# A spectral filter and token MLP, forward and backward: places of some loads, slots and stores changed

## The chip, the core and the metric

The kernel runs on one core of one Trainium2 chip. The metric is the device time of one execution in microseconds (us), here the median of three runs. The engines are PE (matmuls; PEld is its weight load), DVE (vector), ACT (scalar and activations), POOL (it also issues DMAs) and SP (it issues DMAs only).

## What is computed

Forward: a layer norm, a two-dimensional FFT filter over sequence and features, a residual, a second layer norm and a token-mixing MLP, with its residual. Backward: the gradients of all seven inputs that count. The kernel has eight outputs: h2, then the gradients of x, w_r, w_i, w1, b1, w2 and b2 (out_0 to out_7).

```python
def _A_ref(x, w_r, w_i):                      # B, S, D = 1, 2048, 448
    X = jnp.fft.rfft2(x.astype(jnp.float32), axes=(-2, -1))
    X = X * (w_r + 1j * w_i)                  # w_r, w_i: 2048 x 225
    return jnp.fft.irfft2(X, s=(S, D), axes=(-2, -1)).astype(jnp.bfloat16)

def _B_ref(x, w1, b1, w2, b2):                # w1: 2048 x 1792, w2: 1792 x 2048
    h = _layernorm(x, axis=-1)
    u = _gelu(jnp.einsum("bsd,sf->bdf", h, w1) + b1)
    y = jnp.einsum("bdf,fs->bds", u, w2) + b2
    return y.transpose(0, 2, 1)

h = x + _A_ref(_layernorm(x), w_r, w_i)
h2 = h + _B_ref(_layernorm(h), w1, b1, w2, b2)
# and the vector-Jacobian product of all this with grad_out
```

## The kernel before

**Stages, in order of time.** (1) x comes in four pieces of four rows each (`load_x`, L295). Each group is normed (`Norm`, L356 on) and goes through `fft_rows` (L403): DVE folds it into `eo` (L406, L407, L411), PE multiplies it with the table `kf` (L417), ACT or DVE put the result into `zt` (`ev`, L283, L284). (2) Beside this PE has a large, independent product: `dg(j)` (L606), for 14 blocks j of 128, adds up sixteen matmuls (L610) of a block of w2, transposed, with the natural grad_out (`go_nat`). Each block is loaded by a DMA that transposes (`load_w2T`, L325, by `ld_t`, L232) into a ring of four buffers (`w4`), and `dg(j)` asks for the next block at its end. The scheduler puts dg's matmuls between the others to fill PE. (3) `fft_cols` (L436, then L455 and L460 into `xs`), a complex product with w_r and w_i on DVE (`cmul`, L510 to L513, from `w_t`), and the inverse, `ifft_cols` (L534, with the table `hi`; ACT copies one half, L551, DVE adds and subtracts, L553). (4) Rows back (`rows_mid` and `rows_out`, L578 to L590, with `di0` and `kinv`), the residual and the second norm; stores to `hn_d` and `hln_d`. (5) The MLP: w1 in natural layout (L683), the activation and its derivative, w2 in natural layout (L752) with the result h2 stored from L757 on. (6) Backward through w1: sixteen blocks of w1, transposed by DMA into the same ring, L811, and the norm's backward pass (`norm_back`, L770 to L784). (7) The backward FFT with `zt2`, `ds`, `ab2`. Between its steps run the gradients of w2 (`gw2`, from `goT` and `g_t`) and w1 (`gw1`, from `hlnT` and `du_t`), by `halves` (full matmuls at L259, tails on 64 rows at L266). The last four rows of the gradient of w1 run by themselves at the end (L939 on).

**What sets the order.** Each engine and each DMA queue works in its own order; a scheduler makes that order, and semaphores join the queues. `nxt` (L237) chains loads on SP: each is issued behind the one before it in the text. So SP's order in the first part is the order of the calls: x, go_nat, x, go_nat, one w2T, x, x, three w2T, then (L614 to L628) one w2T from `dg(0)`, df1, hf twice, w_t four times, three w2T, hi, di0, kinv, ident. Most stores, and some loads, are issued by POOL (`st`, L229, and L226 with `po`), in their order. `slot(i, ...)` names one of eight large buffers, s0 to s7. A tile in a slot waits until the tile before it there is used up. w2's quarters (`w2c`, L734 to L745) lie in slots 0, 2, 4 and 6; later `g_t` is in 0, `zt2` and then `du_t` in 2, `goT` and then `xs_b` in 4. PSUM has pools m0 and m1 (`ps_mm` takes them in turn) and sp (`ps_sp`), of two, two and four banks.

**The lines that the steps touch.**

```python
    load_x(0)                                   # L298
...
    def ld_t4(out, in_):                        # a transposed load in two DMAs
        ld_t(out[:, 0:3, :], in_[:, 0:384])
        ld_t(out[:, 3, :], in_[:, 320:448])
...
    st(out_7.rearrange("(q h) -> q h", h=NT), gb2b[:])      # L865, on POOL
```

`gb2b` holds sums that ACT makes of the sixteen rows of `go_r` (L766, L768); `go_r` is grad_out again, by rows, in slot 5.

Of the kernel before, what the change touches and what calls it, by code (L numbers as in the profile page):

```python
# [17 lines left out]
P = 128  # L18
S = 2048
D = 448  # L20
DF = 225
F = 1792
NFB = 14
NT = 16
NR = 32
NJ = 16
XW = NJ * DF
# [137 lines left out]
def kernel(  # L165
# [20 lines left out]
    nc = tc.nc  # L186
    ve, ac, po, pe = nc.vector, nc.scalar, nc.gpsimd, nc.tensor
# [7 lines left out]
    def slot(i, shape, name):  # L195
        return big.tile(shape, BF16, tag=f"s{i}", name=name)

    def w4(shape, name):
        return ring.tile(shape, BF16, tag="w4", bufs=4, name=name)
# [15 lines left out]
    def ps_m(k, shape, dtype=F32):  # L215
        return psum.tile(shape, dtype, tag=f"m{k}", bufs=2, name=f"ps_m{k}")

    def ps_mm(shape, dtype=F32):
        turn.append(len(turn) // 2 % 2)
        return ps_m(turn[-1], shape, dtype)  # L220
# [4 lines left out]
    def ld(out, in_, eng=None):  # L225
        return (eng or nc.sync).dma_start(out=out, in_=in_)  # L226

    def st(out, in_, eng=None):
        return (eng or po).dma_start(out=out, in_=in_)  # L229

    def ld_t(out, in_):
        return nc.sync.dma_start(out=out, in_=in_, transpose=True)  # L232
# [4 lines left out]
    def nxt(load, *args):  # L237
        if chain:
            with tc.issue_after(chain[-1].ins):
                chain.append(load(*args))  # L240
        else:
            chain.append(load(*args))

    def ld_t4(out, in_):

        ld_t(out[:, 0:3, :], in_[:, 0:384])
        ld_t(out[:, 3, :], in_[:, 320:448])
# [33 lines left out]
    def ev(out, in_, on):  # L281
        if on == "a":
            return ac.copy(out=out, in_=in_)  # L283
        return ve.tensor_copy(out=out, in_=in_)  # L284
# [4 lines left out]
    def rows(ap):  # L289
        return ap.rearrange("(q h) d -> q h d", h=NT)  # L290
# [4 lines left out]
    def load_x(g):  # L295
        nxt(ld, x[:, 4 * g:4 * g + 4, :], rows(A_x[0])[:, 4 * g:4 * g + 4, :])
# [16 lines left out]
    def table(shape, src, tag=None):  # L313
        t = consts.tile(shape, BF16, name=src, **({"tag": tag} if tag else {}))
        nxt(ld, t[:], hnd[src].ap())
        return t

    def load_w(dst, on):
        for c, w in enumerate((A_w_r, A_w_i)):
            for b in range(2):  # L320
                on(ld, dst[64 * b:64 * b + 64, c, :], by_half(w)[b])
# [3 lines left out]
    def load_w2T():  # L325
        j = len(w2T)
        if j < NFB:
            w2T.append(w4([P, NT, P], "w2T"))
            nxt(ld_t, w2T[j][:], B_w2[j * P:(j + 1) * P, :])


    go_nat = slot(6, [P, NT, D], "go_nat")
    for g in range(2):
        nxt(ld, go_nat[:, 8 * g:8 * g + 8, :],
            grad_out[0].rearrange("(t p) d -> p t d", p=P)[:, 8 * g:8 * g + 8, :])
        if g == 0:
            load_x(1)
    load_w2T()
    load_x(2)
    load_x(3)  # L340
    for j in range(3):
# [61 lines left out]
    def fft_rows(src, zt, g, on, behind=None, twice=False):  # L403
        eo = e4([P, 4, D], "eo")
        a, b = src[:, 4 * g:4 * g + 4, 1:224], src[:, 4 * g:4 * g + 4, 447:224:-1]
        ve.tensor_tensor(out=eo[:, :, 1:224], in0=a, in1=b, op=ALU.add)  # L406
        ve.tensor_tensor(out=eo[:, :, 225:448], in0=a, in1=b, op=ALU.subtract)  # L407
        if twice:
            eo = fold_2(eo, src, g)
        else:  # L410
            ve.tensor_copy(out=eo[:, :, 0:225:224], in_=src[:, 4 * g:4 * g + 4, 0:225:224])  # L411
        for i in range(4):
            h = 4 * g + i
            pz = ps_sp([P, 4, P])
            with tc.issue_after(behind.ins) if behind is not None else nullcontext():
                for c, o in enumerate((0, 113, 226, 322) if twice else (0, 97, 225, 320)):
                    last = pe.matmul(pz[:, c, :], lhsT=eo[:, i, o:o + P], rhs=kf[:, c // 2 * P:c // 2 * P + P],  # L417
                                     start=True, stop=True)
            done = ev(zt[:, :, :, 4 * h:4 * h + 4], pz[:, :, :].rearrange("p c (s k) -> p c s k", k=4), on[i])
        return last, done  # L420
# [185 lines left out]
    def dg(j):  # L606
        pg = ps_m(0, [P, D])
        with tc.issue_after(folded[min(j - 1, 3)][0].ins) if j else nullcontext():
            for t in range(NT):
                pe.matmul(pg[:], lhsT=w2T[j][:, t, :], rhs=go_nat[:, t, :], start=(t == 0), stop=(t == NT - 1))  # L610
        ev(du[:, j, 0:D], pg[:], "a")
        load_w2T()
# [6 lines left out]
        nxt(ld, hf[:, e0:e1], hf_d[:, e0:e1])  # L619
    w_t = slot(4, [P, 2, XW], "w_t")  # L620
    load_w(w_t, nxt)
    for j in range(1, 4):
        dg(j)
    hi = consts.tile([P, 2, NJ, P], BF16, name="hi")
    nxt(ld, hi[:], hnd["hi"].ap().rearrange("p (i j m) -> p i j m", i=2, j=NJ))
    di0 = table([P, 4 * DF], "di0", "di")
    kinv = table([P, 3, P], "kinv")
    ident = table([P, P], "ident")  # L628
    xs = slot(3, [P, 2, XW], "xs")
    fft_cols(zt, df1, xs)  # L630
    cmul(lambda r0, r1: (w_t[:, 0, r0 * DF:r1 * DF], w_t[:, 1, r0 * DF:r1 * DF]), xs, w_t, False)
# [114 lines left out]
    for t0 in range(0, NT, 4):  # L746
# [7 lines left out]
        for i in range(4):  # L754
# [4 lines left out]
            h2_last = st(out_0[0][t * P:(t + 1) * P, :], h2[:])  # L759
# [7 lines left out]
    gb2b = consts.tile([P, NT], BF16, name="gb2b")  # L767
# [22 lines left out]

    w_b = slot(6, [P, 2, XW + 32], "w_b")
    po.memset(w_b[:, :, XW:XW + 32], 0.0)
    zt2 = slot(2, [P, 4, NR, 64], "zt2")
    for h in range(NT):

        if h in (10, 14):
            fft_rows(dh, zt2, h // 4 - 2, "aava", w1_last, True)
        if h == 4:
            goT = slot(4, [P, 4, S], "goT")
            with tc.issue_after(w1T_last.ins):  # L800
                ld_t4(goT[:], grad_out[0])
        if h == 4:
            with tc.issue_after(w1T_last.ins):
                ld(df0[:, 0:452], hnd["df0"].ap())
                ld(di1[:, 0:452], hnd["di1"].ap())
        w1T = w4([P, NFB, P], "w1T")
        with tc.issue_after(chain[-1].ins):
            w1T_last = ld_t(w1T[:], w1Tv[h])
        pd = ps_mm([P, D + 1])
        for j in range(NFB):  # L810
            w1_last = pe.matmul(pd[:], lhsT=w1T[:, j, :], rhs=du[:, j, 0:D + 1], start=(j == 0), stop=(j == NFB - 1))  # L811
        norm_back(pd, True, hln[:, h, :], rstd_h[:, h:h + 1], -(1.0 + LN_EPS) / D, go_r[:, h, :], dh[:, h, :])
# [32 lines left out]
    def fill(n):  # L845
        return [next(others) for i in range(n)]
# [15 lines left out]
        st(dst, sr[:])  # L862

    small_out(out_5.rearrange("(j p) -> j p", p=P), gb1, NFB)
    st(out_7.rearrange("(q h) -> q h", h=NT), gb2b[:])  # L865


    hlnT = slot(1, [P, 4, S], "hlnT")
    ld_t4(hlnT[:], hln_d.rearrange("h q d -> (h q) d"))
    du_t = slot(2, [P, 4, F], "du_t")  # L870
    ld_t4(du_t[:], du_d[:])
    ld_twice(hlnT, w1T_last)
    ld_twice(du_t, w1T_last)
# [1 line left out]
    def gw1(h, ps):  # L875
        s4 = w4([P, F], "s4")
        wdt = (512, 512, 512, 256)
        pws = [ps([P, 512]) for n in range(4)]
        outs = [(pws[n][:, 0:wdt[n]], slice(h * P, (h + 1) * P), slice(512 * n, 512 * n + wdt[n])) for n in range(4)]

        def out():
            for n in range(4):
                cs = slice(512 * n, 512 * n + wdt[n])
                ev(s4[:, cs], pws[n][:, 0:wdt[n]], "a")
                if h == NT - 1:
                    st(rows(out_4)[:, h, cs], s4[:, cs], (nc.sync, po, nc.sync, ac)[n])
            if h < NT - 1:
                st(rows(out_4)[:, h, :], s4[:])

        return outs, out  # L890
# [25 lines left out]
    for h in range(NT):  # L916
        if h + 2 < NT:
            mids.append(rows_mid_twice(ab2, di1, h + 2))
        if h % 4 == 0:
            xr = ring.tile([P, 4, D], BF16, tag="xr", bufs=2, name="xr")  # L920
            with tc.issue_after(h2_4.ins):
                ld(xr[:], rows(A_x[0])[:, h:h + 4, :], po)

            for i in range(h, h + 4):
                po.tensor_scalar(out=xr[:, i - h, :], in0=xr[:, i - h, :], scalar1=rstd_x[:, i:i + 1],
                                 scalar2=nx.nb[:, i:i + 1], op0=ALU.mult, op1=ALU.add)
        with tc.issue_after(mids[-1][1].ins):
            py = rows_out(mids[h][0])
        gx = k1([P, D], "gx")
        norm_back(py, False, xr[:, h % 4, :], rstd_x[:, h:h + 1], -1.0 / D, dh[:, h, :], gx[:])  # L930
        st(rows(out_1[0])[:, h, :], gx[:])
        fill(2)
        if h == 5:
            xs_b = slot(4, [P, 2, XW], "xs_b")
            ld(xs_b[:], xs_d[:])
        if 8 <= h < 14:
            grad_w(R_GROUPS[h - 8])

    for h in range(12, NT, 2):  # L939
        outs, out = gw1(h, ps_mm)  # L940
        outs_2, out_2nd = gw1(h + 1, ps_sp)
        outer(outs, outs_2, hlnT, du_t, False)
        out()
        out_2nd()
# [30 lines left out]
```

## Time and profile before

| what | value |
|---|---|
| runs shown | 359.31, 359.21, 356.01 us |
| median | 359.21 us |
| the profiled execution's own time | 358.12 us |
| its span (first to last instruction) | 356.2 us |
| mean granted PE clock | 0.995 |
| busy: PE, DVE, ACT, POOL | 329.8, 249.1, 208.5, 78.5 us |
| mean DMA rate | 239 GB/s |

How to read what follows. A timeline row gives start, duration, engine, line, operation, output and inputs, the number of instructions merged, and in brackets the idle time before them and what ended it. A row of waits gives the waiting engine and line, what it waited for, the sum, the count and the longest. In a table by stretches each engine has its busy time and, in brackets, its instructions; then come the granted PE clock, the DMA share and GB/s. A `q` behind an engine's name means its instruction queue, which can wait or issue a DMA while the engine does nothing. A DMA's landing is the time from the start of its issue until its data has arrived. Matmuls are pipelined: one of 448 columns lasts 353 ns in a row but the next starts 0.19 us after it.

### The profile page before, as it was taken

To read this page: it belongs to the slowest core of one execution; us is meant where nothing else is said; L and a number is where in the kernel's file an instruction comes from. 1 tells how busy PE (TensorE), PEld (TensorE's weight loads), DVE (VectorE), ACT (ScalarE), POOL (GpSimd) and SP (SyncE) were. 2 spreads that over 40 slices of the span, in tenths; PEclk is the share of its full clock that TensorE was granted. 3 is DMA by queue.
4 is the path that set the end of the run, shared out by engine and by line. 5 is a ranking of instruction groups with operands and counts; after the bars stand their busy time and mean duration, and the time that the engine had idled before them with its cause. 6 is when DMAs were issued, how large, how long until landed. Compare 5 with 4: busy or idle time off the path is not lost.

```text
span 356.2 us, 6196 instructions
## 1 busy us (share of the span) xinstructions
PE 329.8 (93%) x2275; PEld 176.0 (49%) x2275; DVE 249.1 (70%) x582; ACT 208.5 (59%) x432; POOL 78.5 (22%) x135
## 2 busy tenths in 40 slices
PE   0799959999999999999999899999999999999993
PEld 0456635576655555555554355644444454545341
DVE  4884889587646998622217877865798797899910
ACT  3576723447659988200924244488885676877654
POOL 1000000001122110230068000001110134669951
PEclk9999998999999999999999999999999999999999
DMA  8999995999899999999999997999579337777483
GB/s 280 268 238 255 162 231 121 305 261 318 265 280 337 323 284 230 304 338 360 205 205 251 241 203 166 221 190 176 200 164 266 133 145 266 296 257 234 156 298 143
DMA packets 132574, 85.27 MB, mean 239 GB/s; under 512 B 92096, under 2 KB 124224, under 8 KB 132160
## 3 DMA queue, kind: packets, MB, share of 16 engines
q1 hardware_dynamic: 123968, 54.31, 68.0%
q0 software_dynamic: 8288, 30.44, 24.5%
q8 instruction: 18, 0.29, 0.4%
q10 hardware_dynamic: 288, 0.13, 0.2%
q14 instruction: 12, 0.10, 0.1%
HBM read 32.41 MB, written 28.93 MB: 172 GB/s over the span
## 4 chain that ended last, share of the span: by engine, by line
PE 71%; DVE 11%; ACT 6%; DMA 5%; issue 3%; POOL 1%; POOLq 0%; SPq 0%; ACTq 0%; DVEq 0%
PE ps_m L259 14%; PE ps_m L811 10%; PE ps_m L610 7%; PE ps_m L752 6%; PE ps_sp L752 6%; PE ps_m L683 6%; PE ps_sp L683 5%; PE ps_m L266 3%; PE ps_sp L534 2%; DMA w1T<-in_B_w_dram 2%; DMA hi<-tab_hi 2%; PE ps_sp L436 2%; ACT hln L386 2%; ACT zt L283 1%; DVE bs_x L365 1%
## 5 line engine op out<-in xcount | busy, mean ns | idle before, releaser
L283 ACT CAST s<-ps_m 128x512 bf16<-128x512 f32 (+1 forms) x105 | 52.8, 571 | 19.4 <-PE ps_m L266 17.0
L610 PE MATMUL ps_m<-go_nat,w2T 128*128 128x448 bf16 x224 | 50.2, 361 | 0.3 <-DMA w2T<-in_B_w_dram 0.3
L811 PE MATMUL ps_m<-du,w1T 128*128 128x449 bf16 x224 | 43.9, 353 | 1.4 <-DMA w1T<-in_B_w_dram 1.3
L259 PE MATMUL ps_m<-goT,g_t 128*128 128x512 bf16 x168 | 41.2, 381 | 0.0
L229 POOL DMA_DIRECT2D out_dram<-s x30 | 16.3, 542 | 96.7 <-ACT s L283 75.4
L259 PE MATMUL ps_m<-du_t,hlnT 128*128 128x512 bf16 (+1 forms) x168 | 36.0, 353 | 0.7 <-ACT s L283 0.7
L811 PEld LDWEIGHTS <-w1T 128*128 128x128 bf16 x224 | 21.5, 97 | 22.9 <-DMA w1T<-in_B_w_dram 2.7
L752 PEld LDWEIGHTS <-w2c 128*128 128x128 bf16 x224 | 21.9, 98 | 20.5
L683 PEld LDWEIGHTS <-w1c 128*128 128x128 bf16 x224 | 21.7, 98 | 20.2 <-issue 0.5
L752 PE MATMUL ps_m<-gT,w2c 128*128 128x448 bf16 x112 | 30.4, 353 | 0.0
L752 PE MATMUL ps_sp<-gT,w2c 128*128 128x448 bf16 x112 | 30.3, 353 | 0.0
L610 PEld LDWEIGHTS <-w2T 128*128 128x128 bf16 x224 | 21.1, 99 | 17.3 <-issue 2.4
L259 PEld LDWEIGHTS <-hlnT 128*128 128x128 bf16 x192 | 17.6, 98 | 21.1 <-issue 6.7
L757 DVE SCALAR_TENSOR_TENSOR h<-ps_m,b2col,hr 128x448 bf16<-128x448 f32 x8 | 5.1, 680 | 27.5 <-PE ps_m L752 27.5
L553 DVE TENSOR_TENSOR ab<-ps_sp,t 128x512 bf16<-128x512 f32 (+1 forms) x32 | 19.5, 650 | 6.6 <-ACT t L551 6.4
L683 PE MATMUL ps_m<-hln,w1c 128*128 128x448 bf16 x112 | 23.2, 353 | 0.3 <-ACT hln L386 0.3
L259 PEld LDWEIGHTS <-g_t 128*128 128x128 bf16 x168 | 14.6, 98 | 17.7 <-issue 3.8
L775 ACT ACTIVATE nm<-ps_m,rstd_h 128x1 f32<-128x1 f32 x16 | 4.2, 262 | 32.4 <-PE ps_m L811 32.4
L766 ACT ACTIVATE junk<-go_r 128x448 bf16<-128x448 bf16 x16 | 9.2, 577 | 23.6 <-DMA go_r<-in_grad_out_dram 23.1
L683 PE MATMUL ps_sp<-hln,w1c 128*128 128x448 bf16 x112 | 22.7, 353 | 0.0
L229 POOL DMA_DIRECT2D hn_d<-x x4 | 2.2, 548 | 82.4 <-DVE x L639 82.4
L484 DVE TENSOR_TENSOR gu<-ps_sp,gi 128x450 bf16<-128x450 f32 (+3 forms) x16 | 9.9, 618 | 12.7 <-ACT gi L481 12.7
(157 smaller groups left out, 649.6 us busy)
## 6 DMA issues: line engine op xcount, KB each, us to landing
w1c<-in_B_w_dram SPq DMA_DIRECT2D x7, 1024.0 KB, 10.2
w2c<-in_B_w_dram SPq DMA_DIRECT2D x8, 896.0 KB, 12.9
out_dram<-s POOLq DMA_DIRECT2D x14, 512.0 KB, 4.1
out_dram<-s POOLq DMA_DIRECT2D x15, 448.0 KB, 3.3
xs_d<-xs SPq DMA_DIRECT2D x1, 1800.0 KB, 7.4
xs_b<-xs_d SPq DMA_DIRECT2D x1, 1800.0 KB, 9.0
x<-in_A_x_dram SPq DMA_DIRECT2D x4, 448.0 KB, 4.4
go_nat<-in_grad_out_dram SPq DMA_DIRECT2D x2, 896.0 KB, 7.1
```

What stands on the lines that cost most here:

```text
L229: return (eng or po).dma_start(out=out, in_=in_)
L259: last = pe.matmul(ps, lhsT=lhs[:, c, a], rhs=rhs[:, c, b], start=opens and c == 0, stop=not opens and c == 2)
L266: last = pe.matmul(ps, lhsT=lhs[k, 3, a], rhs=rhs[k, 3, b], start=opens, stop=not opens)
L283: return ac.copy(out=out, in_=in_)
L386: ac.activation(out=self.dst[:, h, :], in_=self.src[:, h, :], func=ACT.Identity, scale=self.rstd[:, h:h + 1], bias=nb[:, i:i + 1])
L484: ve.tensor_tensor(out=in_order(g[:, first:, :]), in0=by_k(pt[0][:, first:, :]), in1=by_k(gi[:, first:, :]), op=op)
L553: ve.tensor_tensor(out=place(a, 4 * j, 4 * j + 2 * n), in0=view(pt[0][:, :, 0:n, :]), in1=view(t1[:, :, 0:n, :]), op=op)
L610: pe.matmul(pg[:], lhsT=w2T[j][:, t, :], rhs=go_nat[:, t, :], start=(t == 0), stop=(t == NT - 1))
L683: pe.matmul(pu[:], lhsT=wc[:, h, o:o + P], rhs=hln[:, h, :], start=(h == 0), stop=(h == NT - 1))
L752: pe.matmul(p2[i][:], lhsT=w2c[t0 // 4][:, j, i * P:(i + 1) * P], rhs=gT[:, j, :], start=(j == 0), stop=(j == NFB - 1))
L766: ac.activation(out=junk[:], in_=go_r[:, h, :], func=ACT.Copy, accum_out=gb2[:, h:h + 1])
L811: w1_last = pe.matmul(pd[:], lhsT=w1T[:, j, :], rhs=du[:, j, 0:D + 1], start=(j == 0), stop=(j == NFB - 1))
```

## The change

Five places.

1. The load of w2's first block is called before go_nat's loads, so on SP it stands directly behind x's first piece.
2. The loads of hi, di0, kinv and ident are called before dg(1) to dg(3), so on SP they stand ahead of the three w2T that those ask for, and directly behind w_t.
3. Slots 2 and 4 change places for goT, zt2, du_t and xs_b.
4. The store of gb2b is issued by POOL behind the last store of h2.
5. At the end, the casts of rows 14 and 15 of the gradient of w1 alternate between ACT and DVE. Row 14 is stored in two parts from SP. Row 15 is stored in four, three from SP and one from ACT; before, row 14 and one part of row 15 went from POOL. In the last four rows the two PSUM pools change places.

The scheduler moves other instructions with these: three matmuls of dg(0) come ahead of the first L417 on PE; a first L534 comes ahead of the last four matmuls of dg(4), and the next 31 come behind five matmuls of dg(5), not sixteen.

```diff
     go_nat = slot(6, [P, NT, D], "go_nat")
+    load_w2T()
     for g in range(2):
         nxt(ld, go_nat[:, 8 * g:8 * g + 8, :], ...)
         if g == 0:
             load_x(1)
-    load_w2T()
     load_x(2)
...
     load_w(w_t, nxt)
-    for j in range(1, 4):
-        dg(j)
     hi = consts.tile([P, 2, NJ, P], BF16, name="hi")
     nxt(ld, hi[:], hnd["hi"].ap().rearrange("p (i j m) -> p i j m", i=2, j=NJ))
     di0 = table([P, 4 * DF], "di0", "di")
     kinv = table([P, 3, P], "kinv")
     ident = table([P, P], "ident")
+    for j in range(1, 4):
+        dg(j)
...
-    zt2 = slot(2, [P, 4, NR, 64], "zt2")
+    zt2 = slot(4, [P, 4, NR, 64], "zt2")
...
-            goT = slot(4, [P, 4, S], "goT")
+            goT = slot(2, [P, 4, S], "goT")
...
-    st(out_7.rearrange("(q h) -> q h", h=NT), gb2b[:])
+    with tc.issue_after(h2_last.ins):
+        st(out_7.rearrange("(q h) -> q h", h=NT), gb2b[:])
...
-    du_t = slot(2, [P, 4, F], "du_t")
+    du_t = slot(4, [P, 4, F], "du_t")
...
-                ev(s4[:, cs], pws[n][:, 0:wdt[n]], "a")
+                ev(s4[:, cs], pws[n][:, 0:wdt[n]], "a" if h < NT - 2 else "avav"[n])
                 if h == NT - 1:
-                    st(rows(out_4)[:, h, cs], s4[:, cs], (nc.sync, po, nc.sync, ac)[n])
-            if h < NT - 1:
+                    st(rows(out_4)[:, h, cs], s4[:, cs], (nc.sync, nc.sync, nc.sync, ac)[n])
+                elif h == NT - 2 and n % 2:
+                    cs = slice(1024 * (n // 2), min(1024 * (n // 2) + 1024, F))
+                    st(rows(out_4)[:, h, cs], s4[:, cs], nc.sync)
+            if h < NT - 2:
                 st(rows(out_4)[:, h, :], s4[:])
...
-            xs_b = slot(4, [P, 2, XW], "xs_b")
+            xs_b = slot(2, [P, 2, XW], "xs_b")
...
-        outs, out = gw1(h, ps_mm)
-        outs_2, out_2nd = gw1(h + 1, ps_sp)
+        outs, out = gw1(h, ps_sp)
+        outs_2, out_2nd = gw1(h + 1, ps_mm)
```

## The prediction

> **What bounds the kernel now.** I read the page's shares first (PE busy for 93% of the span), then PE's waits, the SP queue's timeline, PE's timeline, a table by stretches, and the tail. PE's waits on other engines and transfers are three places (others are under 0.8 us):
>
> ```profile
> PE ps_sp L417 <- DVE eo L411: 10.9, 2, 10.7
> PE ps_sp L534 <- DMA hi<-tab_hi: 4.2, 1, 4.2
> PE ps_m L811 <- DMA w1T<-in_B_w_dram: 1.3, 1, 1.3
> ```
>
> The first is the start (x, its norm and fold); the other two are loads that come late. Why `hi` is late stands in the SP queue:
>
> ```profile
> 27.90 1.23 SPq L226 DMA_DIRECT2D w_t<-in_A_w_i_dram  x2
> 29.23 15.41 SPq L232 DMA_TRANSPOSE w2T<-in_B_w_dram  x3
> 44.69 0.57 SPq L226 DMA_DIRECT2D hi<-tab_hi  x1
> 47.14 14.60 SPq L232 DMA_TRANSPOSE w2T<-in_B_w_dram  x3
> ```
>
> Three transposes hold the queue for 15.41 us. In the view of the tile w2T the first stands on the queue for 10.14 us, to 39.4: the copies ahead of it (w_t, issued at 28.54, landing after 11.0) land at 39.5. So a transpose leaves only when the copies before it have landed, and whatever is queued behind it waits. On PE:
>
> ```profile
> 45.51 2.63 PE L610 MATMUL ps_m<-go_nat,w2T 128*128 128x448 bf16 x13
> 52.34 2.12 PE L534 MATMUL ps_sp<-hi,w_t 64*128 64x128 bf16 x33 [4.20 <-DMA hi<-tab_hi]
> 54.39 2.01 PE L610 MATMUL ps_m<-go_nat,w2T 128*128 128x448 bf16 x7
> ```
> ```profile
> 47.90:52.30 4.40, 0.24 (x2) 0.09 (x1) 4.02 (x8) 0.53 (x1) 0.00 (x0) 0.97 1.27 249
> 52.30:55.60 3.30, 3.26 (x37) 2.22 (x37) 1.42 (x3) 1.17 (x2) 0.00 (x0) 0.52 0.85 189
> 55.60:57.00 1.40, 1.40 (x13) 0.56 (x11) 1.40 (x4) 0.00 (x0) 0.00 (x0) 1.00 1.22 242
> ```
>
> In the table the number behind POOL's is the granted clock. After the 4.20 us wait PE runs at 0.52 for 3.3 us: another 3.3 x 0.48 = 1.6 us of work is lost. The late `hi` costs 5.8, not 4.2. The w1T wait is short and leaves no slow stretch (70 matmuls take 13.84 us behind it, 13.76 before it). POOL's queue ahead of it:
>
> ```profile
> 155.80 0.54 POOL L226 DMA_DIRECT2D xr<-in_A_x_dram  x1
> 180.47 0.55 POOL L229 DMA_DIRECT2D out_dram<-gb2b  x1 [24.12 <-ACT gb2b L768]
> 190.92 2.19 POOL L229 DMA_DIRECT2D out_dram<-h  x4
> ```
>
> One small store keeps POOL waiting for 24.12 us, with a load of x and eight stores of h behind it. The tail:
>
> ```profile
> 349.39 1.89 ACT L283 CAST s<-ps_sp 128x512 bf16<-128x512 f32 x4
> 351.31 0.37 ACTq L229 DMA_DIRECT2D out_dram<-s  x1
> ```
> ```profile
> L970 POOLq DRAIN x3: 46/93/4613, 350.8 to 355.9; - x3
> L970 SPq DRAIN x3: 7/7/13, 354.4 to 355.7; - x3
> ```
>
> PE's last matmul ends at 350.63; the last store (3.0 to landing) lands at 354.3 and SP is done at 354.4, but POOL's drain, begun at 350.8, lasts 4.61, to 355.4, and the span ends 0.8 later.
>
> **The change, part by part.** The sum is made against the profiled execution, 358.12 us (span 356.2 and 1.9 around it). That is 1.1 under the median of the three runs, 359.21, and 2.1 over the fastest.
>
> 1. *The first w2T ahead of go_nat.* One transpose moves past two copies of go_nat and one of x on SP. Bytes and holds stay the same in number: it now holds for x's first piece (issued 0.74, landing after 3.8) instead of for go_nat. In the built program three matmuls of the first dg stand ahead of the first fft_rows on PE. They need go_nat's first half: transpose away at about 4.5, about 2 to land, 896 KB (2.4 us: its halves and x's pieces now land 2.4 and 1.2 apart), so 9 to 10. Three matmuls at the slow start (up to 0.58 each) end at 10.2 to 11.7; fft_rows wants PE at 10.66. Delay 0 to 1.0, of which the DVE and ACT chain behind (the chain of waits runs through it up to 26.2) hides some. x's last pieces land at most 0.7 earlier. The three matmuls do free 0.6 us of PE later, but fft_rows's last group still waits for DVE at 26.2, as before. Ends -0.7 and +1.0; I take +0.2, near a pass-through of a delay of some tenths.
>
> 2. *hi, di0, kinv, ident ahead of three w2T.* Four issues (0.57 + 0.42 + 0.43 + 0.79 = 2.2 us of SP) move past three transposes; 1.4 MB now lies between w_t and block 5. What goes: 4.2 + 1.6 = 5.8. What is late next: PE's built order has one L534 matmul, the last four of block 4, eight L455, then five matmuls of block 5, then the other 31 L534. (a) That first L534 is due at 43.6 and needs hi. w_t lands at 39.5; hi took 5.1 behind the transposes before it (47.2 to 52.3); its 1.05 MB at the 314 GB/s of 48 to 50 are 3.3: 42.8 to 44.6. I take a wait of 0.2. (b) Block 5 leaves when ident has landed, 1.1 behind hi, at about 44.5, and lands 2.1 (block 8: 53.2 to 55.4) to 3.4 (block 5: 39.4 to 42.8) later. I take 47.3, nearest to block 5's own row. PE is there at 45.1: a new wait of 2.2, bounds 0.6 to 4.0. Blocks 6 to 10 follow some 2.5 apart and PE uses 3.0 us for each, so nothing more waits. Gain 5.8 - 2.4 = 3.4; DVE, idle for only 2.23 + 1.52 + 0.39 = 4.1 from 52 to 69, caps it at 4.1, and its adds (0.69 each) will not fit perfectly: I take -3.2, ends -4.1 and +0.8 (waits of 1.0 and 4.0 and the slow clock again, 6.6, against 5.8). What follows is PE work without gaps to 141, so the gain stays; the loads of w1c2, w1c3 and w2c0 wait for PE or hn_d, and shift with it.
>
> TensorE: Matmul & The Clock Gate (Part 1: The HAM clock gate) in the Trainium skill says that the clock halves after an idle window of about 3.4 us; by that rule a wait of 2.2 keeps the full clock, and one of 4.0 does not. This trace agrees as far as it goes, 4.20 against 1.30.
>
> 3. *The slot swap for goT, zt2, du_t, xs_b.* goT no longer needs the third quarter of w2c to be used up. That is at 173.3; goT's first issue stands at 175.42, behind g_t, which is behind go_r. Its place in the queue does not change, so 0. The other three take over a slot from the same predecessor as before. The cover is g_t's place in the queue: without it the earlier slot would count.
>
> 4. *gb2b's store behind the last h store.* One issue (0.55) goes from POOL's 180.47 past a load of xr and twelve h stores. Nobody on PE waits for POOL. But 448 KB of xr and 896 KB of h leave up to 24 us earlier, the h buffers come free (DVE waited 3.89 for them), and w1T number 5, which took 6.9 to land among the h stores (192.0 to 198.9), has less beside it. PE lost 1.5 here (1.30 and 0.2). Against it: the same bytes now lie beside go_r, g_t and goT, on which w1T depends in the queue. Ends -1.5 and +5.1 (1.38 MB at 268 GB/s, the rate of 186 to 188, when such traffic ran nearly alone). I take -1.0, near the 1.5, since all these bytes but the last stores lay ahead of w1T 5 before too.
>
> 5. *The last stores.* Casts of the last two rows alternate ACT and DVE. The last one, 256 wide, starts when PE ends and takes 0.42 on DVE: 351.1 instead of 351.3. POOL's last DMA is now row 13's (345.9), and its 4.61 drain ends by 351. The span then ends with the last landing: 354.1 + 0.1 + 0.8 = 355.0 against 356.2. I take -1.2; ends -1.3 and +0.5, if five stores on SP (0.35 each) queue up. The swapped psum pools touch no wait on PE: it has none from 338 on.
>
> Sum: +0.2 - 3.2 + 0 - 1.0 - 1.2 = -5.2, so 352.9 us.
>
> **The rivals.**
>
> *A. The wait only changes its name.* Block 5 lands at 49 instead of 47.3, PE waits about 4 and falls to the slow clock again: part 2 gives 0, and the time is 358.1 - 2.0 = 356.1. For it: block 5's slow 3.4, and table loads that landed as far as 3.2 apart for 512 KB (hf). Against it: w_t's and hi's copies would be streaming back to back.
>
> *B. POOL's freed traffic makes w1T late (the other side).* w1T 4 landed at 194.8, just when PE wanted it. If xr and the h stores push go_r, g_t and goT back by the full 5.1, PE waits 5.1 there and runs slowly after it (1.6): 358.1 + 0.2 - 3.2 - 1.2 + 6.7 = 360.6. It decides from about 4 us of delay on. Against it: those bytes then no longer lie beside goT's landing.
>
> *C. The last drain stays last.* If POOL's drain waits for something else than its own stores, only the earlier cast and a cheaper issue are left: -0.2 and 0.54 - 0.35 = 0.2. The tail gives 0.4, the time is 353.7. For it: SP's drains are 0.01, so a drain of 4.61 is unlike the rest. DMA: Bandwidth & Descriptors (Issuing engines are not separate DMA queues) in the Trainium skill says that the engine that starts a DMA changes only its issue time, which speaks against this part; the trace of before has no second tail to compare with.
>
> **How the numbers follow.** Chances: forecast 0.54 (its own range 350.5 to 355.5), A 0.22, B 0.10, C 0.14. 350.0 to 357.5 holds the forecast, A and C with the bounds of part 1; it leaves out B and the best ends of all parts together, under 0.2. About 1% is what a measurement of this kernel can tell from no change: its three runs lie 0.9% apart. From 359.21 that is 355.6 and 362.8. Under 355.6: nine tenths of the forecast and seven tenths of C, 0.58. Over 362.8: the worst of B, 0.06. The rest, 0.36.
>
> **What would show it.** Right: no PE wait for `hi` above 1 us, a wait of 1 to 3 us at L610 for w2T near 45 with the clock at 1.00 behind it; the L534 run starting near 48 instead of 52.34; no `gb2b` in POOL's long waits and none of DVE's for out_dram<-h; w1T's wait on PE below 0.5; POOL's long drain begun near 346. Wrong: a slow-clock stretch between 45 and 55, a longer wait at L811, or fft_rows starting after 11.5 with L436 after 30.5.

## The result, and the profile after

| comparison with the kernel before | median | median of before beside it | ratio, 95% interval |
|---|---|---|---|
| the change, 22 runs | 354.22 us | 359.45 us | 0.986 (0.983 to 0.9891) |
| the change once more, 12 runs, another chip | 354.56 us | 355.53 us | 0.9938 (0.9895 to 0.9981) |

By the ratios the change makes the kernel faster, by 1.4% (5.0 us) in the first comparison and by 0.6% (2.2 us) in the second. The two intervals do not overlap. The profiled execution of the changed kernel took 352.96 us, its span is 351.1 and its mean clock 1.000. The forecast was 352.9. The ratios leave out runs over 1.5% above the fastest of their kernel (8 of the 22, 4 of the 12), and so are not the quotient of the medians; one profile below, that of the fourth part alone, is of such a run (361.13 us).

Milestones of the two profiled executions, from the timelines (in the changed kernel the lines at the end are five higher, L975 for L970; the names here are those of before):

| milestone | before | after | difference |
|---|---|---|---|
| L436 first starts | 29.75 | 30.97 | +1.22 |
| L534, 128th ends | 67.85 | 65.46 | -2.39 |
| L683 first starts | 97.23 | 96.33 | -0.90 |
| L811 first starts | 183.91 | 183.00 | -0.91 |
| L811 last ends | 230.70 | 228.15 | -2.55 |
| L259 last (PE's end) | 350.63 | 347.66 | -2.97 |
| end of the span | 356.17 | 351.13 | -5.04 |

The order of SP after the change, in its timeline (start, duration, what is issued):

```profile
27.20 1.71 SPq L226 DMA_DIRECT2D w_t<-in_A_w_i_dram  x2
28.95 0.58 SPq L226 DMA_DIRECT2D hi<-tab_hi  x1
29.58 0.43 SPq L226 DMA_DIRECT2D di<-tab_di  x1
30.94 0.32 SPq L226 DMA_DIRECT2D kinv<-tab_kinv  x1
33.87 0.32 SPq L226 DMA_DIRECT2D ident<-tab_ident  x1
35.77 25.15 SPq L232 DMA_TRANSPOSE w2T<-in_B_w_dram  x6
```

hi now leaves at 28.95 and lands at 44.18 (before: 52.30). PE's waits after the change:

```profile
PE ps_m L610 <- DMA go_nat<-in_grad_out_dram: 10.6, 1, 10.6
PE ps_sp L417 <- DVE eo L411: 2.3, 2, 1.8
PE ps_m L455 <- DVE gv L484: 1.3, 1, 1.3
PE ps_m L610 <- DMA w2T<-in_B_w_dram: 1.2, 1, 1.2
```

The waits for hi and for w1T are gone from the list. The wait at the start now ends with go_nat, 10.6, and 2.3 more follow at L417, where before it was 10.9 at L417 alone. New are a wait at L455 for a sum of DVE (gv, L484), 1.3, and one for w2T, 1.2. DVE makes gv late because in its order the complex product (L511) stands ahead, and that waits for w_t, which landed at 42.06 (39.58 before). The row of L511, before and after:

```profile
39.68 0.86 DVE L511 TENSOR_TENSOR t_i<-xs,w_t 128x1350 bf16<-128x1350 bf16 x1 [0.31 <-DMA w_t<-in_A_w_i_dram]
```
```profile
42.15 0.86 DVE L511 TENSOR_TENSOR t_i<-xs,w_t 128x1350 bf16<-128x1350 bf16 x1 [1.77 <-DMA w_t<-in_A_w_i_dram]
```

PE's timeline after (in brackets the idle time before, and what ended it):

```profile
46.03 0.23 PE L534 MATMUL ps_sp<-hi,w_t 64*128 64x128 bf16 x1
...
49.02 1.12 PE L610 MATMUL ps_m<-go_nat,w2T 128*128 128x448 bf16 x5 [1.22 <-DMA w2T<-in_B_w_dram]
50.07 1.06 PE L534 MATMUL ps_sp<-hi,w_t 64*128 64x128 bf16 x31
```

The 31 matmuls of L534 take 1.06 us; before, 33 took 2.12, on the half clock. At the end, the drains of POOL and SP (durations shortest/median/longest in ns, then first to last start):

```profile
L975 POOLq DRAIN  x3: 46/93/6150, 343.0 to 350.9; - x3
L975 SPq DRAIN  x3: 7/7/13, 350.3 to 350.6; - x3
```

POOL's long drain now starts at 343.0 and is over before SP's, 350.3. So most signs that the prediction named for "right" are in this one profile: no wait for hi, one for w2T of 1.22 at full clock (at 49, not near 45), none above 0.5 for w1T, POOL's drain begun before 346. Against it, L534's run starts at 50.07 and not near 48, and L417 at 11.71 with L436 at 30.97, which it named for "wrong". The experiments ask whether the differences of this one pair of profiles come from the change.

### The profile page after: what moved, and what is told of

It reads as the page before. It is cut to its first block, busy times and chain, and to the rows that moved or that the text cites. A ratio compares the mean times of both kernels' runs of the same rounds, so it can differ in the third digit from the quotient of the medians.

```text
span 351.1 us, 6182 instructions
## 1 busy us (share of the span) xinstructions
PE 326.5 (93%) x2258; PEld 175.5 (50%) x2275; DVE 250.3 (71%) x586; ACT 207.9 (59%) x428; POOL 78.3 (22%) x133
## 4 chain that ended last, share of the span: by engine, by line
PE 69%; DVE 13%; DMA 8%; SPq 5%; ACT 3%; issue 2%; DVEq 0%; ACTq 0%
PE ps_m L259 16%; PE ps_m L811 9%; PE ps_sp L752 6%; PE ps_m L752 6%; PE ps_m L683 6%; PE ps_sp L683 6%; PE ps_m L610 6%; DMA w_t<-in_A_w_i_dram 4%; SPq L232 3%; PE ps_m L266 3%; DMA w2T<-in_B_w_dram 3%; DVE ab L553 2%; SPq L226 2%; DVE t_i L511 2%; DVE t_r L510 2%
## 5 line engine op out<-in xcount | busy, mean ns | idle before, releaser
L610 PE MATMUL ps_m<-go_nat,w2T 128*128 128x448 bf16 x224 | 49.5, 356 | 12.0 <-DMA go_nat<-in_grad_out_dram 10.6
L811 PE MATMUL ps_m<-du,w1T 128*128 128x449 bf16 x224 | 43.6, 353 | 0.1
L259 PE MATMUL ps_m<-goT,g_t 128*128 128x512 bf16 x158 | 39.5, 380 | 0.7 <-issue 0.5
L229 POOL DMA_DIRECT2D out_dram<-s x28 | 15.2, 544 | 97.5 <-ACT s L283 76.2
L259 PE MATMUL ps_m<-du_t,hlnT 128*128 128x512 bf16 (+1 forms) x161 | 35.4, 352 | 1.1 <-ACT s L283 0.5
L610 PEld LDWEIGHTS <-w2T 128*128 128x128 bf16 x224 | 20.8, 98 | 27.7 <-DMA w2T<-in_B_w_dram 8.8
L811 PEld LDWEIGHTS <-w1T 128*128 128x128 bf16 x224 | 21.7, 97 | 21.1 <-DMA w1T<-in_B_w_dram 0.5
L683 PEld LDWEIGHTS <-w1c 128*128 128x128 bf16 x224 | 21.8, 98 | 20.5 <-issue 0.5
L259 PEld LDWEIGHTS <-hlnT 128*128 128x128 bf16 x192 | 17.6, 98 | 21.0 <-issue 6.5
L259 PEld LDWEIGHTS <-g_t 128*128 128x128 bf16 x168 | 14.6, 98 | 17.7 <-issue 3.8
L683 PE MATMUL ps_m<-hln,w1c 128*128 128x448 bf16 x112 | 23.0, 353 | 0.3 <-ACT hln L386 0.3
L683 PE MATMUL ps_sp<-hln,w1c 128*128 128x448 bf16 x112 | 22.7, 352 | 0.0
L484 DVE TENSOR_TENSOR gu<-ps_sp,gi 128x450 bf16<-128x450 f32 (+3 forms) x16 | 9.9, 618 | 12.7 <-ACT gi L481 12.7
```

The costliest lines, as they stand in the source:

```text
L259: last = pe.matmul(ps, lhsT=lhs[:, c, a], rhs=rhs[:, c, b], start=opens and c == 0, stop=not opens and c == 2)
L484: ve.tensor_tensor(out=in_order(g[:, first:, :]), in0=by_k(pt[0][:, first:, :]), in1=by_k(gi[:, first:, :]), op=op)
L683: pe.matmul(pu[:], lhsT=wc[:, h, o:o + P], rhs=hln[:, h, :], start=(h == 0), stop=(h == NT - 1))
```

## The experiments

Each kernel has one profile, and times beside the kernel before on the same chip: 12 runs beside 35 of before, in the last comparison 6 beside 11, and in two cases a single run, as said there. Four kernels are the kernel before with one part of the change alone; the slot swap was not tried alone.

**The first part alone.**

```diff
     go_nat = slot(6, [P, NT, D], "go_nat")
+    load_w2T()
...
-    load_w2T()
     load_x(2)
```

> The kernel before with its first step alone: the first w2T directly behind x's first piece. Theory: three cold matmuls and the later go_nat hold the first rows' FFT, so L417 first starts at about 11.7 instead of 10.66 and L436 first at 31.0 instead of 29.75, and w_t lands later as well (42.1 instead of 39.6). The transposes behind w_t then leave later too, so hi lands about 2 later and nothing is absorbed: 1.2 to 2.5 us slower than the kernel before. Rival 1 (the prediction's step 1): +0.2, a pass-through of some tenths. Rival 2: the delay is absorbed by the wait for hi, whose queue does not move: L436 first is late by 1.2, L534 first still at 52.3, the time the same.

Measured: 357.04 against 356.29, ratio 1.0015 (0.9972 to 1.0059). PE's timeline, the start, and one row of its waits:

```profile
9.67 1.28 PE L610 MATMUL ps_m<-go_nat,w2T 128*128 128x448 bf16 x3 [9.67 <-DMA go_nat<-in_grad_out_dram]
10.74 1.91 PE L417 MATMUL ps_sp<-kf,eo 128*128 128x128 bf16 x16
```
```profile
PE ps_sp L534 <- DMA hi<-tab_hi: 1.1, 1, 1.1
```

go_nat's half landed a microsecond earlier than in the profile of the whole change, and L417 and L436 stand at 10.74 and 29.98, within 0.25 of the kernel before. The theory's 1.2 falls. The wait for hi is 1.1, although nothing behind w_t was moved. So the 4.20 in the profile of before is one sample of a wait that varies.

**The second part alone.**

```diff
-    for j in range(1, 4):
-        dg(j)
     hi = consts.tile([P, 2, NJ, P], BF16, name="hi")
...
     ident = table([P, P], "ident")
+    for j in range(1, 4):
+        dg(j)
```

> The kernel before with its second step alone: hi, di0, kinv, ident ahead of three w2T. Theory: the wait for hi (4.2) and the slow clock behind it (1.6) go, a wait for block 5 of w2T of 1 to 2.5 comes, and the deferred matmuls of L610 are made up for later: L683 first 2 to 3 earlier than 97.2, the time 2 to 3 us shorter. Rival 1 (the prediction's size): L683 first and the time 3.2 or more earlier. Rival 2 (the wait only changes its name): PE waits about 4 for w2T, the clock is halved again, and the time is the same within 0.5.

Measured: 355.49 against 356.29, ratio 0.9997 (0.9963 to 1.0031): no difference that this can tell, and at most 0.4% either way. PE's timeline:

```profile
44.41 0.23 PE L534 MATMUL ps_sp<-hi,w_t 64*128 64x128 bf16 x1
...
46.57 1.12 PE L610 MATMUL ps_m<-go_nat,w2T 128*128 128x448 bf16 x5 [0.39 <-DMA w2T<-in_B_w_dram]
47.75 1.31 PE L534 MATMUL ps_sp<-hi,w_t 64*128 64x128 bf16 x31
...
50.14 0.23 PE L534 MATMUL ps_sp<-hi,w_t 64*128 64x128 bf16 x1 [0.79 <-DVE w_t L512]
```

The mechanism works: hi is there, the first L534 stands at 44.41, the waits are 0.39 and 0.79 and the clock is full. L683 starts at 94.72, which is 2.5 before that of the profile of before (97.23), but only 0.9 and 1.2 before those of the fourth and fifth part alone (95.57, 95.92), whose front is that of the kernel before, and 1.4 behind that of the first part alone (93.29), where hi was not moved. A step that shows 2.5 us in a pair of profiles gave none in 12 runs.

**The fourth part alone.**

```diff
-    st(out_7.rearrange("(q h) -> q h", h=NT), gb2b[:])
+    with tc.issue_after(h2_last.ins):
+        st(out_7.rearrange("(q h) -> q h", h=NT), gb2b[:])
```

> The kernel before with its fourth step alone: gb2b's store behind the last store of h2. Theory: w1T's block 5 no longer lands among the stores of h; PE's wait for w1T (1.3) is gone and L811's stage is 1.3 to 1.7 shorter than 46.79, the time 1.3 to 1.9 us shorter. Rival 1: in the whole change it was the slot swap that made this gain; then the wait of 1.3 stays and the time is the same within 0.3. Rival 2: the freed traffic makes another block of w1T late: a wait of over 1.3 at L811, the time not shorter.

Measured: 358.43 against 356.29, ratio 1.006 (1.0015 to 1.0106): slower, by 0.6%. Its profile is of a run that took 361.13. PE's waits; SP's timeline in the kernel before; and SP's timeline here:

```profile
PE ps_m L811 <- DMA w1T<-in_B_w_dram: 4.1, 1, 4.1
PE ps_sp L534 <- DMA di<-tab_di: 1.7, 1, 1.7
```
```profile
162.08 13.24 SPq L232 DMA_TRANSPOSE g_t<-gT_d  x2
175.42 14.13 SPq L232 DMA_TRANSPOSE goT<-in_grad_out_dram  x2
189.65 11.22 SPq L232 DMA_TRANSPOSE w1T<-in_B_w_dram  x4
```
```profile
153.09 7.27 SPq L226 DMA_DIRECT2D go_r<-in_grad_out_dram  x2
161.03 18.45 SPq L232 DMA_TRANSPOSE g_t<-gT_d  x2
179.58 12.75 SPq L232 DMA_TRANSPOSE goT<-in_grad_out_dram  x2
192.43 8.13 SPq L232 DMA_TRANSPOSE w1T<-in_B_w_dram  x4
```

The two transposes of g_t stay on the queue for 18.45 us (13.24 in the profile of before), and goT and w1T behind them are late: w1T leaves at 192.43, 10.2 behind L811's first matmul, where it was 5.7 before. POOL issues four stores of h at 162.67, which land at 173.0 to 175.9; the first g_t is off the queue at 176.6. That is rival B's mechanism, and the theory of a gain falls. This profile shows it at its strongest: in the three profiles of faster runs with the fourth part (the change twice, and the change without its first part) the pair of g_t holds the queue for 14.73 to 15.09, and PE does not wait for w1T. The second row of waits is hi's wait again, put down to di: hi landed at 50.03.

**The fifth part alone.**

```diff
-                ev(s4[:, cs], pws[n][:, 0:wdt[n]], "a")
+                ev(s4[:, cs], pws[n][:, 0:wdt[n]], "a" if h < NT - 2 else "avav"[n])
...
-                    st(rows(out_4)[:, h, cs], s4[:, cs], (nc.sync, po, nc.sync, ac)[n])
+                    st(rows(out_4)[:, h, cs], s4[:, cs], (nc.sync, nc.sync, nc.sync, ac)[n])
```

with the stores of row 14 on SP and the two PSUM pools swapped, as in the change.

> The kernel before with its fifth step alone: the casts and stores of the last two rows, and the two PSUM pools swapped. Theory: POOL's last drain begins some 7 us earlier, and the span ends 3.3 to 3.6 behind PE's last matmul instead of 5.6: 2.0 to 2.3 us shorter. Rival 1 (the last drain waits for something else than POOL's own stores): 0.4 shorter. Rival 2 (the prediction's size, landings of 3.0): 1.2 shorter.

Measured: 353.88 against 356.29, ratio 0.9922 (0.9873 to 0.997). The drains:

```profile
L974 POOLq DRAIN  x3: 46/97/4695, 344.8 to 352.8; - x3
L974 SPq DRAIN  x3: 7/7/13, 352.2 to 352.5; - x3
```

POOL is done before SP, and the span ends 3.47 behind PE's last matmul. This distance is the steadiest number of the study: 5.53 to 5.55 in the four profiles without the fifth part, 3.47 or 3.48 in seven with it, 3.76 and 3.90 in two more.

The traces split the 2.07. Before, the last landing comes 3.68 behind PE's last matmul and the end of the span 1.86 behind that landing; in the fifth part alone it is 2.25 and 1.22. So 1.43 is an earlier last landing (the last store, from ACT, lands in 1.76 us instead of 3.00, and is issued 0.19 earlier) and 0.64 is that POOL's drain no longer comes last. In all fourteen profiles that drain ends 1.4 to 1.8 behind the landing of POOL's own last DMA. Why the last stores land faster was not taken apart.

**The whole change again, and without the first, the fourth, or both.** All four ran on one chip. The edits take back the diffs above.

> The changed kernel as it is, beside three variants of it. The four parts alone came to ratios of 1.0015, 0.9997, 1.006 and 0.9922 against the kernel before, product 0.999; the whole came to 0.986 in its first runs. Theory 1 (parts add up, and the first result was helped by how late the loads happened to land in those runs): about 0.995 to 1.0. Theory 2 (parts work together: without the fourth part's wait for g_t and goT, or with the slot swap, it costs nothing): 0.986 again. The mean clock of its runs shows how many slow stretches each had; under theory 1 some runs have 0.985 or less, from a wait for w1T of over 3.4.

> The changed kernel without its fourth part (gb2b's store back ahead of POOL's load of xr). Theory (the freed stores of h land beside go_r and hold the transposes g_t and goT, and behind them w1T): goT's first issue again 8 to 10 ahead of L811's first matmul instead of 6.2, no run with a clock under 0.99, median 1 to 3 us below the whole change. Rival (the fourth part gave the 1.64 that the first profile showed): median 1.5 above the whole change, with a wait for w1T of 1.0 or more in the profile.

> The changed kernel without its first part (go_nat's first half again ahead of w2T's first block). Theory (the 1.22 by which L436 came later in the profile of the changed kernel is the first part's cost): L436 first at 29.7 to 30.0, w_t landed at 39 to 40, median 1.0 to 1.5 below the whole change. Rival (that profile's loads happened to land late; the first part costs nothing): L436 between 29.7 and 30.8 in either, medians within 0.5. With part 1 alone L436 stood at 29.98.

> The second, third and fifth part without the first and fourth. If both the theory on the fourth part and the rival on the first hold: the same as without the fourth part within 0.5, and 1 to 3 below the whole change. If the first part does cost 1.2: another 1.2 below that. If the fourth part gives 1.6: above the whole change by 0.4 to 1.6.

| kernel | median | ratio, 95% interval |
|---|---|---|
| the whole change | 354.56 us | 0.9938 (0.9895 to 0.9981) |
| without the fourth part | 353.84 us | 0.9957 (0.9918 to 0.9995) |
| without the first part | 356.2 us | 0.9975 (0.9923 to 1.0027) |
| the second, third and fifth part only | 352.73 us | 0.9938 (0.9905 to 0.997) |

The whole's 0.9938 lies between the theories, and its interval leaves out 0.986. The intervals of the four kernels overlap, so by these ratios neither the first nor the fourth part can be told from nothing inside the whole.

For the first part, the theory's start came true, L436 at 31.77 in the whole and at 29.94 without it, but not its gain: w_t landed at 41.10 and 42.64, and the 128th matmul of L534 ended at 64.90 and 66.05, so the kernel that started earlier was the later one there. Without the fourth part the median is 0.7 below that of the whole, not 1 to 3. For the fourth part, the traces bear out what it does to the queue: without it goT's first issue stands 9.4 and 9.6 ahead of L811's first matmul, with it 6.0 and 6.1. What that costs PE varies. L811's stage takes 44.9 where no block is late. With the fourth part it took 44.9 twice, 45.2, 50.3 and 51.6; without it 44.9 twice, 46.4 to 46.9 four times, 47.9 and 49.2 (in these counts the kernel that leaves out stores is not included). The 1.64 that the stage lost between the two first profiles lies inside this spread. The mean clocks of the runs are a further count: one stretch of 3.4 us at half clock takes 0.005 off the mean, and of the 24 runs with the fourth part on this chip 11 have 0.995 or less, of the 24 without it one. That speaks against the fourth part, as its times alone do, but only one run of each kernel has a trace, so where the other slow stretches came from is not shown. The 0.994 clock of the profile with only three parts comes from a wait for w1T of 2.5 (stretch, busy PE, then the others, granted clock, DMA share, GB/s):

```profile
192.30:194.80 2.50, 0.03 (x1) 0.00 (x0) 2.39 (x7) 0.99 (x2) 0.21 (x1) 1.00 1.21 101
194.80:196.00 1.20, 1.16 (x7) 0.60 (x7) 1.13 (x3) 0.00 (x0) 0.00 (x0) 1.00 1.21 151
196.00:199.40 3.40, 3.40 (x11) 1.39 (x10) 0.83 (x3) 0.22 (x1) 0.00 (x0) 0.51 1.18 291
```

**What holds the transpose.** The whole change, with the stores of rows 4 to 7 of h2 left out.

```diff
-            h2_last = st(out_0[0][t * P:(t + 1) * P, :], h2[:])
+            if not 4 <= t < 8:
+                h2_last = st(out_0[0][t * P:(t + 1) * P, :], h2[:])
```

> The changed kernel without the stores of rows 4 to 7 of h2; these rows are left out of the output. They are the four stores that the fourth part lets POOL issue beside go_r. Theory (they hold the transpose g_t, since it leaves when the copies ahead of it have landed): the first g_t is gone from the queue 10 to 11 before L811's first matmul, as without the fourth part (10.2, 11.5, 10.6, 11.1), and not 5.6 to 8.5 before it as with it. Rival (xr's second load or the stores of rows 8 to 11 hold it, or the slot): it stays at 5.6 to 8.5.

Measured: one run, 352.25 us. SP's timeline:

```profile
160.14 13.33 SPq L232 DMA_TRANSPOSE g_t<-gT_d  x2
173.56 13.71 SPq L232 DMA_TRANSPOSE goT<-in_grad_out_dram  x2
187.37 7.13 SPq L232 DMA_TRANSPOSE w1T<-in_B_w_dram  x3
```

The first g_t is off the queue 10.1 before L811's first matmul, as without the fourth part (10.2 and more), where the profiles with it have 5.6 to 8.5. The pair holds the queue for 13.33, where those have 14.73 to 18.45. xr's loads and the stores of rows 8 to 11 are still there, so these four stores are what holds the transpose, as far as one run can show it.

**One piece of row 15 on POOL again.**

```diff
-                    st(rows(out_4)[:, h, cs], s4[:, cs], (nc.sync, nc.sync, nc.sync, ac)[n])
+                    st(rows(out_4)[:, h, cs], s4[:, cs], (nc.sync, po, nc.sync, ac)[n])
```

> The changed kernel with one of the four pieces of row 15 issued by POOL, as before the change. Theory (POOL's long last drain begins when its last DMA has been issued, and lasts 4.6 or more from there): POOL's drain begins 0.1 to 0.5 behind PE's last matmul and ends the span, 4.8 to 5.6 behind that matmul instead of 3.47. Rival (the drain depends on all of POOL's traffic, or the gain came from the cast on DVE and the shorter landings): 3.4 to 4.0 behind it.

Measured: one run, 358.26 us. The drains, and PE's longest wait for a load:

```profile
L975 POOLq DRAIN  x3: 46/93/3901, 351.7 to 356.2; - x3
L975 SPq DRAIN  x3: 7/7/13, 354.8 to 355.9; - x3
```
```profile
PE ps_m L811 <- DMA w1T<-in_B_w_dram: 3.6, 1, 3.6
```

POOL's drain starts 0.1 behind PE's last matmul, as before the change, and ends the span, 4.75 behind that matmul: more than the 3.4 to 4.0 of the rival, just under the theory's 4.8. It lasts 3.90, not the theory's 4.6 or more, and ends 1.77 behind the landing of POOL's last store. One store on POOL costs 1.28 of the 2.07: 0.82 is the drain, 0.46 a later last landing (2.71 behind PE's last matmul, not 2.25). The rival's shorter landings are real too: before, that landing came 3.68 behind. The 3.6 at L811 is the wait for w1T once more.

**Another place for hi.** The third and fifth part, and hi with the three tables behind the first of the three w2T.

```diff
-    for j in range(1, 4):
-        dg(j)
+    dg(1)
     hi = consts.tile([P, 2, NJ, P], BF16, name="hi")
...
     ident = table([P, P], "ident")
+    for j in range(2, 4):
+        dg(j)
```

> Parts 3 and 5, and the second part in another place: hi, di0, kinv and ident behind the first of the three w2T instead of ahead of all three. Theory (in the second part the wait for hi is replaced by waits for w2T, w_t and the product behind it of 1.6 to 3.3 in all, since block 5 leaves only when ident has landed): block 5 lands at 41 to 43 as in the kernel before, hi at 43.5 to 45.5, PE waits under 1.0 for either, L436 first to L683 first is 63.0 to 64.0 (with the second part 64.0 to 67.0), and the time is 0.5 to 1.5 below that of parts 2, 3 and 5. Rival (the second half of the wait is DVE's product, which no order of loads moves): 64.0 or more, the time the same within 0.5. Rival 2: hi again waits behind a transpose, L534 waits over 1.5 for it, and the clock is halved behind it.

> Parts 2, 3 and 5 once more, beside the kernel with hi behind one w2T. It came to 0.9938 (0.9905 to 0.997), 2.2 us; the fifth part's 2.07 is in every trace. Theory (the fifth part is nearly all of it): 0.993 to 0.997, span end 3.4 to 3.5 behind PE's last matmul. Rival (the second part brings another 2): 0.988 to 0.990.

Measured on one chip, with before at 359.48: 353.42, ratio 0.9823 (0.9764 to 0.9881), and for the parts 2, 3 and 5 356.86, ratio 0.9875 (0.9814 to 0.9936). The intervals overlap; the order is the expected one. SP and PE of the new kernel:

```profile
28.45 11.51 SPq L232 DMA_TRANSPOSE w2T<-in_B_w_dram  x1
40.01 0.58 SPq L226 DMA_DIRECT2D hi<-tab_hi  x1
```
```profile
42.26 0.26 PE L455 MATMUL ps_m<-gv,hf 128*64 128x225 bf16 x1 [0.58 <-DVE gv L484]
...
45.89 0.21 PE L534 MATMUL ps_sp<-hi,w_t 64*128 64x128 bf16 x1 [0.62 <-DMA hi<-tab_hi]
...
48.65 1.06 PE L534 MATMUL ps_sp<-hi,w_t 64*128 64x128 bf16 x31
```

Block 5 lands at 43.48 and hi at 45.85, 0.5 and 0.35 later than expected. No wait in this stage is over 0.62, and L436 to L683 takes 63.50, less than in any of the nine profiles with the second part as it is (63.99 to 66.97). The first part alone, where hi stands behind all three w2T, took 63.30 though, so one profile does not show that the new place is better. The kernel has the lowest ratio of the study, from five of its six runs. The second kernel's 0.9875, from three of six, lies near the rival's 0.988 to 0.990: it points to more than the fifth part's 0.6% where the kernel before takes 359.5. Its span ends 3.76 behind PE's last matmul, not 3.4 to 3.5.

## Why the prediction was right, and where it was not

The time came out 1.3 above the forecast, inside its own range, but the sum is right only as a sum, and that is luck. The profiled pair moved by 5.04 where 5.2 was forecast: the first step cost 1.0 more than said, the second brought 1.1 less, the fourth 0.6 more and the fifth 0.9 more, and 0.4 between L811's end and PE's end was in no term. Over several executions one of the five steps failed (gb2b's store) and two were mis-sized (hi and the last stores).

1. *The first w2T ahead of go_nat (+0.2).* The first profile said +1.22. Over all profiles L436 starts at 30.73 in the mean with it (six) and at 30.08 without (eight), +0.65, and the times show nothing. The +1.22 lies outside the bounds of -0.7 and +1.0; neither it nor the +0.2 can be called the cost.

2. *hi ahead of three w2T (-3.2).* This is the mis-sized term. In the pair of first profiles the stretch from L436 to L683 went from 67.48 to 65.36, -2.1: the 4.20 went, the slow clock cost about 0.9 (L534's first to 128th takes 15.51 there and 14.58 in the first part alone, without a slow stretch), not 1.6, and waits of 1.31, 1.22 and 0.33 came. The prediction had 0.2 and 2.2. It kept w_t's landing at 39.5 although hi now follows directly behind: the last piece of w_t landed at 39.95 to 42.64 in the nine profiles with the second part as it is, at 38.16 to 39.58 in the four without, and the work of DVE that waits for it was in no term. Counted from L436, L534's 128th matmul ended 3.6 earlier, but the scheduler had pushed eight matmuls of L610 behind it: from there to L683 it is 30.86 or 30.87 where it was 29.38 to 29.40, in every profile with the second part as it is (eight times 0.19 is 1.5). Whoever takes L534's shift for the gain counts 1.48 that are given back by L683. The larger error is the basis: hi's wait was 4.20, 2.21, 1.67 and 1.08 in four executions with the same loads behind w_t. Over all profiles, L436 to L683 takes 64.86 in the mean with the second part (nine, 63.99 to 66.97) and 65.41 without (four, 63.30 to 67.48). Alone it gave a ratio of 0.9997 (0.9963 to 1.0031). Rival A's result for this part, that a wait only changes its name, was near the truth on that chip, though not by a wait of 4 for w2T and not with a slow clock.

3. *The slot swap (0).* goT's issue stayed behind g_t, as said (176.84 after 175.42). Not tried alone.

4. *gb2b's store (-1.0).* Failed. The first profile seemed to confirm it, with -1.64, but alone it is slower by 0.1 to 1.1%, and the wait it was to remove came back as 4.1 and 3.6. The 1.5 that it was to win was a sample too: without the fourth part L811's stage took 44.9 to 49.2. It counted eight stores of h as freed; in the profile after all twelve that stood behind gb2b's leave 9 to 19 us earlier. The step looked at what lay beside w1T's block 5 and not at what lay ahead of the transposes before it. Rival B had the mechanism; its condition, 4 us of delay, is met in some executions and not in others.

5. *The last stores (-1.2).* Mis-sized in the right direction: -2.07. The landings were taken as 3.0 and took 1.74 to 2.66 in the profile after. So the larger share of the gain, 1.43, is the earlier last landing, for which the sum had 0.2; POOL's drain, for which it had 1.0, gave 0.64. Rival C falls: POOL's drain goes with POOL's own last store. It is the part whose price changed least from profile to profile, 1.6 to 2.1 us, which is 0.5 to 0.6%.

The 2.2 of the second comparison is about what the fifth part gives alone; that it is the fifth part is inferred from the size. The 5.0 of the first is that and about 3 more. Where the kernel before took 359.5, the parts 2, 3 and 5 gained 1.25%, where it took 355.5, 0.62%, with intervals that overlap. In the former case all of its 11 runs had a mean clock of 0.995 or less, in the latter 15 of 35 had 0.996 or more. That fits a wait for hi that is long on some occasions and short on others; those runs have no traces, so it stays an inference, and the cause of the other 3 us is open. The part of the first comparison's gain that is due to the slot swap is open.

## What to carry to other kernels

A wait for a DMA that one profile shows is one sample: here the same load was late by 1.1 to 4.2 us. Before a wait is summed as gain, look at other executions for its spread. Measure the gain between two milestones that both kernels have, the second one behind all work that the scheduler put off, not at the instruction that moved. Where a queue carries transposes, count the copies of all queues that will be under way when they want to leave: here stores that POOL could issue earlier kept a transpose on SP's queue. When a load is moved ahead, ask what it shares the time of landing with.

## What the runs showed of the hardware

*Short waits can halve the clock.* In the fourteen profiles, behind the start, PE waited six times for 1.67 us or more (1.67, 2.21, 2.51, 3.60, 4.06 and 4.20), and each time a stretch of 3.4 us at half clock came, once one of 6.8. In the fifth part alone it came with the end of the wait of 2.21, in the fourth part alone 2 us behind the wait of 1.67:

```profile
48.70:51.00 2.30, 0.09 (x2) 0.06 (x1) 2.27 (x4) 0.53 (x1) 0.00 (x0) 0.96 0.96 356
51.00:54.00 3.00, 3.00 (x36) 2.10 (x36) 2.76 (x7) 1.17 (x2) 0.00 (x0) 0.50 1.11 221
```
```profile
48.10:50.10 2.00, 0.33 (x3) 0.09 (x1) 1.97 (x5) 0.53 (x1) 0.00 (x0) 1.00 0.91 345
50.10:52.10 2.00, 1.73 (x35) 1.21 (x35) 2.00 (x4) 1.07 (x2) 0.00 (x0) 0.99 1.27 254
52.10:55.20 3.10, 3.10 (x14) 1.08 (x13) 3.10 (x7) 0.00 (x0) 0.00 (x0) 0.50 0.94 187
```

The waits of 1.53 and less left the clock at 1.00, also 1.33 and 1.53 that ended 3.8 us apart (the change without its first part). TensorE: Matmul & The Clock Gate (Part 1: The HAM clock gate) of the Trainium skill has a half clock after an idle window of about 3.4 us, and the prediction took from it that a wait of 2.2 would be harmless. So the measurement differs from the rule as the prediction used it.

*The issuing engine can cost more than its issue time.* DMA: Bandwidth & Descriptors (Issuing engines are not separate DMA queues) of the Trainium skill puts the difference down to issue time. At the end of the program POOL's last drain ends 1.4 to 1.8 us behind the landing of POOL's last DMA, in all fourteen profiles, while SP's first drain at the end is done 0.1 to 0.5 us behind the last landing of all. With one store of row 15 on POOL the span ended 1.28 later behind PE's last matmul, 0.82 of it behind the last landing. So the measurement differs from that section here.
